# Attention and MLP in one kernel: the last chunk of w_out requested behind batch 1's normalise, batch 1's v ahead of it, and its products behind the kv products

## The chip, the cores and the metric

One core of a Trainium2 chip. The time is the device time of one execution in microseconds; below are medians of a few executions, and ratios are from runs of both kernels in the same rounds, so not quite the ratio of the medians that I quote. "First tile" is tokens 0 to 511, "tile 1" the next 512. Times inside a trace count from the start of its span. In the traces PE is TensorE, DVE VectorE, ACT ScalarE, POOL GpSimd and SP SyncE; "the clock" is the share of its full clock that TensorE was granted.

## The reference

Linear attention for 8 batches (8 heads, 576 positions, head dimension 64), then an MLP with a "snake" activation on the 4608 tokens:

```python
q_s = softmax(q, axis=-1);  k_s = softmax(k, axis=2)          # plain exp and sum in the kernel
kv  = einsum('bhsd,bhse->bhde', k_s, v)
x   = einsum('bhsd,bhde->bhse', q_s, kv)                      # -> (4608, 512)
h = x @ w_in                                                  # (4608, 2048)
g = h + sin(alpha * h)**2 / (alpha + 1e-9)
out = g @ w_out                                               # (4608, 512)
```

## The kernel before

Every tile of 512 tokens takes 64 products for `h`, an activation in between, and 64 products for `out`. In between stand the small attention products of the next batch. TensorE runs in program order; `take(os, n)` puts the next n of the first tile's 64 `out` products at that place in the order. w_out comes in four chunks of four blocks each; chunk c feeds products 16c+1 to 16c+16. It is cast from float32 to bfloat16 on its way and requested from GpSimd's queue; q, k and v come through Sync's.

```python
def load_wout(c):
    nc.gpsimd.dma_start(out=wout[:, 4*c:4*c+4, :], in_=wout_v[:, 4*c:4*c+4, :])
...
    GP_CP(win[:, :, 0:256], wf)              # first 256 columns of w_in, cast on GpSimd
...
late = {6: lambda: load("q", q, 1, halves=True, gate=DVE_CP), 8: lambda: load_wout(2),
        10: lambda: load_wout(3), 13: lambda: load("k", k, 1, halves=True, gate=DVE_CP)}
...                                          # 16 slots of the first tile; late[n] behind slot n
take(os, 10)
xp = ps_e.tile([128, 4, P], F32, name="xp", tag="a")
for c in range(4):
    attn_chunk(0, c, 8, 9, xp[:, c])
ACT_CP(xT[:, :, 8 * P:9 * P], xp)
take(os, 36)
exp_q(1)
load("v", v, 1, halves=True)
load_batch(2)                                # q, k, v of batch 2, Sync's queue
norm_q(1, [GP, V])                           # half on GpSimd, half on DVE
exp_k(1)
for ii in range(2):
    q_transpose(1, ii, ps_e, DVE_CP)         # TensorE, copies on DVE
cast_v(1, [ACT_CP, DVE_CP])
...
take(os, 8)
kv_mm(1, 0, ps_e, split=True)
kv_norm(1, 0, 1)
take(os, 2)
kv_mm(1, 1, ps_e, split=True)
kv_norm(1, 1, 2)
take(os, 1)
...                                          # two xp pairs with take(os, 2) behind each; the rest; tile 1
```

The softmax here doesn't subtract the row's maximum and nothing guards it: scores larger than these inputs give would overflow.

## Time and profile before

| | before |
|---|---|
| time, median (range) | 289.55 us (289.01 to 289.61) |
| span of the profiled run | 287.6 us |
| TensorE busy, mean granted clock | 95%, 0.997 |
| first tile's first w_in product / first w_out product | 16.23 / 30.05 us |
| last w_out chunk requested / landed | 28.40 / 38.76 us |
| batch 1's v landed (two halves) | 41.33, 42.71 us |
| tile 1's first w_in product | 47.76 us |

A busy TensorE is not a streaming one (each matmul's 379 ns overlap the next; the pitch of a 512-column product is 0.216 us), so gaps are read from start to start. Most of the lines are in the prediction; this is the one of tile 1:

```profile
47.76 3.62 PE L234 MATMUL hp<-xT,win 128*128 128x512 bf16 x16
```

### The profile page before, as it was taken

What the parts mean: (1) busy time and instruction counts of PE and PEld (TensorE: products, weight loads), DVE (VectorE), ACT (ScalarE), POOL (GpSimd) and SP (SyncE); (2) the same over time, 40 slices, a digit from 0 to 9 for tenths busy, and PEclk for the clock granted to TensorE, in tenths of its full rate; (3) what the DMA queues carried; (4) which work ended last, traced back from release to release, by engine and by line L of the source; (5) the groups of instructions that cost most, each with busy time, mean ns of one, the idle gap of its engine ahead of it and who ended that gap; (6) DMA issues with size and microseconds to landing.
All of it is one profiled execution on the core that took longest, in us unless ns stands there. A gap on an engine that the chain in (4) does not pass through costs nothing.

```text
span 287.6 us, 4234 instructions
## 1 busy us (share of the span) xinstructions
PE 273.7 (95%) x1542; PEld 130.8 (45%) x1570; DVE 188.6 (66%) x280; ACT 227.2 (79%) x321; POOL 79.8 (28%) x73
## 2 busy tenths in 40 slices
PE   2889999999999999999999999999999999999994
PEld 1434454445454445444544454445444444444443
DVE  3867595889958667856776677757674555555412
ACT  5799775999479999899889988998877777777500
POOL 0679420675775571005300440032000000000000
PEclk9999999999999999999999999999999999999998
DMA  7999999935899957129910990116011111111142
GB/s 257 341 205 245 267 401 407 309 150 161 196 153 404 392 187 128 38 43 368 275 32 22 331 333 8 38 39 136 19 39 36 36 36 39 36 38 36 46 103 73
DMA packets 37893, 46.03 MB, mean 160 GB/s; under 512 B 15968, under 2 KB 21360, under 8 KB 37872
## 3 DMA queue, kind: packets, MB, share of 16 engines
q1 hardware_dynamic: 33392, 41.69, 47.5%
q0 software_dynamic: 4288, 3.93, 8.4%
q8 instruction: 12, 0.20, 0.3%
q10 hardware_dynamic: 192, 0.14, 0.2%
q14 instruction: 9, 0.07, 0.1%
HBM read 36.71 MB, written 9.44 MB: 160 GB/s over the span
## 4 chain that ended last, share of the span: by engine, by line
PE 83%; DMA 5%; POOL 4%; DVE 3%; issue 2%; SPq 1%; ACT 1%; POOLq 0%
PE hp L234 36%; PE op L254 34%; PE hp L254 4%; DMA st_w<-in_moe_w_in_dram 3%; POOL s L244 3%; PE kvp L157 2%; PE xp L206 2%; PE hh L234 1%; DMA qT<-qn 1%; PE op L538 1%; PE op L234 1%; ACT s L240 1%; DVE g L250 1%; DVE qs L144 1%; SPq L94 1%
## 5 line engine op out<-in xcount | busy, mean ns | idle before, releaser
L250 DVE SCALAR_TENSOR_TENSOR g<-s,inva_sb,hp 128x512 bf16<-128x512 f32 x130 | 96.2, 746 | 64.2 <-ACT s L242 54.2
L234 PE MATMUL hp<-xT,win 128*128 128x512 bf16 x512 | 129.2, 379 | 1.2 <-POOL win L320 0.6
L254 PE MATMUL op<-wout,g 128*128 128x512 bf16 x479 | 121.9, 379 | 1.1 <-issue 0.5
L240 ACT ACTIVATE s<-hp,alpha_sb 128x512 f32<-128x512 f32 x130 | 87.7, 682 | 25.8 <-PE hp L234 25.0
L234 PEld LDWEIGHTS <-win 128*128 128x128 bf16 x576 | 56.1, 98 | 68.3 <-POOL win L320 1.1
L254 PEld LDWEIGHTS <-g 128*128 128x128 bf16 x560 | 54.1, 98 | 61.7 <-issue 0.8
L242 ACT ACTIVATE s<-s 128x512 f32<-128x512 f32 x112 | 70.5, 630 | 3.5
L146 POOL TENSOR_TENSOR qn<-qe,qs 128x1152 bf16<-128x1152 bf16 x12 | 25.3, 2126 | 74.3 <-DVE qs L140 63.1
L244 POOL TENSOR_TENSOR s<-s 128x512 f32<-128x512 f32 x29 | 30.5, 1062 | 22.2 <-ACT s L240 21.6
L260 DVE COPY o<-op 128x512 f32<-128x512 f32 (+2 forms) x33 | 22.1, 670 | 9.7 <-PE op L254 5.8
L117 ACT ACTIVATE ke<-st_k 128x1152 bf16<-128x1152 f32 x16 | 17.9, 1151 | 3.0 <-DMA st_k<-in_k_dram 3.0
L117 ACT ACTIVATE qe<-st_q 128x1152 bf16<-128x1152 f32 x16 | 17.8, 1155 | 2.4 <-DMA st_q<-in_q_dram 2.3
L139 DVE TENSOR_REDUCE qs<-qe 128x36 f32<-128x2304 bf16 x5 | 12.8, 2553 | 8.7 <-ACT qe L117 8.6
L131 POOL CAST vb<-st_v 128x1152 bf16<-128x1152 f32 x12 | 13.6, 1162 | 10.1 <-DMA st_v<-in_v_dram 10.1
L254 PE MATMUL hp<-wout,g 128*128 128x512 bf16 x62 | 14.8, 379 | 0.2 <-issue 0.2
L209 DVE CAST xT<-xp 128x512 bf16<-128x512 f32 (+1 forms) x18 | 13.4, 743 | 0.0
L144 DVE TENSOR_REDUCE qs<-qe 128x18 f32<-128x1152 bf16 x6 | 8.0, 1330 | 4.6 <-ACT qe L117 4.6
L157 PE MATMUL kvp<-vb,ke 64*128 64x130 bf16 x288 | 9.9, 217 | 0.3 <-ACT vb L310 0.3
L117 ACT ACT_TABLE_LOAD x7 | 9.0, 1283 | 1.3 <-PEq L552 1.2
L157 PEld LDWEIGHTS <-ke 64*128 64x128 bf16 x288 | 8.2, 93 | 3.9 <-ACT s L242 1.3
L234 PE MATMUL hh<-xT,win 128*128 128x512 bf16 x39 | 9.4, 379 | 0.1
L206 PE MATMUL xp<-qT,kbd 128*128 128x256 bf16 (+1 forms) x40 | 8.2, 286 | 0.4 <-DVE xT L209 0.3
(68 smaller groups left out, 117.3 us busy)
## 6 DMA issues: line engine op xcount, KB each, us to landing
out_dram<-o SPq DMA_DIRECT2D x70, 128.0 KB, 2.4
st_q<-in_q_dram SPq DMA_DIRECT2D x6, 1152.0 KB, 6.6
st_k<-in_k_dram SPq DMA_DIRECT2D x6, 1152.0 KB, 8.5
st_v<-in_v_dram SPq DMA_DIRECT2D x6, 1152.0 KB, 10.3
st_q<-in_q_dram SPq DMA_DIRECT2D x4, 576.0 KB, 5.1
st_k<-in_k_dram SPq DMA_DIRECT2D x4, 576.0 KB, 7.1
wout<-in_moe_w_out_dram POOLq DMA_DIRECT2D x4, 512.0 KB, 9.6
st_v<-in_v_dram SPq DMA_DIRECT2D x3, 576.0 KB, 9.2
```

The source lines that it names most:

```text
L117: nc.scalar.activation(dst[:, :, ii * 128:(ii + 1) * 128].rearrange("p j (x d) -> p x j d", x=2), src[:, ii::2], AX.Exp)
L131: engs[ii](vv[:, 2 * ii:2 * ii + 2, :, 0:D], staged["v", b][:, ii::2])
L146: engs[ii % len(engs)].tensor_tensor(qn[:, ii].rearrange("p j (x d) -> p j x d", x=2), qe[:, ii], part.unsqueeze(3).to_broadcast([128, J, ...
L157: nc.tensor.matmul(kvp[:, e, ii * 130:(ii + 1) * 130], ke[r, j, ii * 128:(ii + 1) * 128], vt[r, j, ii * 130:(ii + 1) * 130], start=(j == 0 ...
L206: nc.tensor.matmul(xp[:, e, 0:n], kt[:, e, ii], qT[:, ii, j0:j1, e * 64:(e + 1) * 64], start=True, stop=True)
L234: nc.tensor.matmul(hp, win[:, ki, ni * 128:(ni + 1) * 128], xT[:, ki, t * MF:(t + 1) * MF], start=(ki == 0), stop=(ki == 3))
L240: nc.scalar.activation(s, hp, AX.Sin, scale=alpha_sb[:, ni:ni + 1])
L242: nc.scalar.activation(s, s, AX.Square)
L244: nc.gpsimd.tensor_tensor(s, s, s, op=ALU.mult)
L250: nc.vector.scalar_tensor_tensor(G[t][:, ni], in0=s, scalar=inva_sb[:, ni:ni + 1], in1=hp, op0=ALU.mult, op1=ALU.add)
L254: nc.tensor.matmul(acc, G[t][:, ni, j * 128:(j + 1) * 128], wout[:, ni, :], start=(ni == 0), stop=(ni == nN - 1))
L260: eng(o[:, cols], acc)
```

## The change

Its author wanted batch 1's v, which the kv products need, ahead of the last w_out chunk in the memory traffic. The chunk's request therefore moves from slot 10 to behind the normalise on GpSimd, and its products move behind the kv products, to give it time. With it come three smaller parts: the w_in cast in two halves, 20 products in place of 10 ahead of the small `xp` group (whose copy goes to DVE), and v's cast ahead of the copies of qT on DVE.

```diff
-    GP_CP(win[:, :, 0:256], wf)
+    for n in range(2):
+        GP_CP(win[:, :, n * 128:n * 128 + 128], wf[:, :, n * 128:n * 128 + 128])
@@
-                10: lambda: load_wout(3), 13: lambda: load("k", k, 1, halves=True, gate=DVE_CP)}
+                13: lambda: load("k", k, 1, halves=True, gate=DVE_CP)}
@@
-        take(os, 10)
+        take(os, 20)
...
-        ACT_CP(xT[:, :, 8 * P:9 * P], xp)
-        take(os, 36)
+        DVE_CP(xT[:, :, 8 * P:9 * P], xp)
+        take(os, 26)
...
         norm_q(1, [GP, V])
+        load_wout(3)
         exp_k(1)
+        cast_v(1, [ACT_CP, DVE_CP])
         for ii in range(2):
             q_transpose(1, ii, ps_e, DVE_CP)
-        cast_v(1, [ACT_CP, DVE_CP])
...
-        take(os, 8)
-        kv_mm(1, 0, ps_e, split=True)
-        kv_norm(1, 0, 1)
         take(os, 2)
-        kv_mm(1, 1, ps_e, split=True)
-        kv_norm(1, 1, 2)
-        take(os, 1)
+        for ii in range(2):
+            kv_mm(1, ii, ps_e, split=True)
+            kv_norm(1, ii, ii + 1)
```

## The prediction

> **What bounds the kernel now.** I read the page first: share of each engine, then the chain that ended last.
>
> ```profile
> PE 273.7 (95%) x1542; PEld 130.8 (45%) x1570; DVE 188.6 (66%) x280; ACT 227.2 (79%) x321; POOL 79.8 (28%) x73
> ...
> PE 83%; DMA 5%; POOL 4%; DVE 3%; issue 2%; SPq 1%; ACT 1%; POOLq 0%
> ```
>
> TensorE carries the end. Busy is not peak, so I checked the pitch in the timeline: 512-column products start 0.216 us apart. From the first product of w_in (16.23) to the end, gaps over that pitch are few (those of exactly one pitch are lost records): 0.44 us before the `xp` products at 32.74, about 0.3 to 0.5 us each near 74 and 94 us. Nothing else is to be had after 16.2 us. So any new wait of TensorE adds in full, and the most that the change can win is what it takes out between 15 and 48 us. That stretch, in the timeline (start, length, instruction, idle before it and its releaser):
>
> ```profile
> 28.40 0.80 POOL L110 DMA_DIRECT2D wout<-in_moe_w_out_dram  x1
> ...
> 30.05 2.41 PE L254 MATMUL hp<-wout,g 128*128 128x512 bf16 x10
> ...
> 32.74 0.28 PE L214 MATMUL xp<-qT,kbd 128*128 128x64 bf16 x4 [0.28 <-DVE g L250]
> ...
> 32.86 7.93 PE L254 MATMUL hp<-wout,g 128*128 128x512 bf16 x35
> ...
> 35.94 1.35 DVE L144 TENSOR_REDUCE qs<-qe 128x18 f32<-128x1152 bf16 x1 [2.59 <-ACT qe L117]
> ...
> 37.76 2.13 POOL L146 TENSOR_TENSOR qn<-qe,qs 128x1152 bf16<-128x1152 bf16 x1 [5.33 <-DVE qs L145]
> ...
> 41.35 1.17 ACT L131 CAST vb<-st_v 128x1152 bf16<-128x1152 f32 x1 [0.20 <-DMA st_v<-in_v_dram]
> ...
> 43.49 0.69 PE L157 MATMUL kvp<-vb,ke 64*128 64x130 bf16 x18
> ...
> 46.68 1.24 PE L254 MATMUL hp<-wout,g 128*128 128x512 bf16 x5
> ```
>
> The reader is to see that the last chunk of w_out is requested at 28.40, and that the products of it (49 to 64 of the first tile) start about 42.1, well after it landed at 38.76. Tile 1's first w_in product is at 47.76. The DMA engines meanwhile are full (window sums; last columns clock, DMA share, GB/s):
>
> ```profile
> 33.00:35.00 2.00, 2.00 (x11) 0.87 (x9) 0.35 (x1) 1.91 (x3) 0.00 (x0) 1.00 1.23 219
> 38.00:40.00 2.00, 1.95 (x10) 0.90 (x10) 1.93 (x3) 1.18 (x2) 1.89 (x1) 1.00 1.05 411
> 42.00:44.00 2.00, 2.00 (x26) 1.00 (x23) 2.00 (x4) 1.97 (x3) 0.00 (x0) 1.00 1.04 412
> ```
>
> 219 GB/s is a stretch in which w_out (counted as written, in bf16) has the engines; 411 is q, k and v. They stay full until batch 2's v lands at 51.50. And what a w_out request takes from issue to landing:
>
> ```profile
> L110 POOL DMA_DIRECT2D wout<-in_moe_w_out_dram x4: 774/786/801, 17.3 to 28.4; - x4
> ...
> DMA to landing us min/median/max: 8.6/9.6/10.5
> ```
>
> **What the Trainium skill says.** "DMA: Bandwidth & Descriptors", Queues, rings and completion order: each DMA engine goes round-robin between queues, a packet at a time. The packet records agree once both queues are under way: from about 29.8 and again 34.9 us, packets of GpSimd's queue and of Sync's alternate one by one on an engine, a pair in 0.186 us. The same page (Latency and other measured facts) gives about 1 us to the first byte on GpSimd's path; here the first packet came 4.0 us after the issue began at 8.75, and about 4.1 us after the issue at 25.60, behind a full Sync queue both times, so I use 4.1. "TensorE: Matmul & The Clock Gate", Part 1: after an idle window of about 3.4 us TensorE falls to half clock and needs about 3.4 us of work to come back. The trace agrees: after the last product (283.9) the granted clock is 1.00 to 286 and 0.59 on average in 286 to 287 (half from 286.2), and the first warm-up matmuls (5.74 us on) have a pitch of 0.427 us, and 0.216 only from 9.7, 4.0 us later.
>
> **The change part by part.**
>
> (1) *w_in copy in two halves.* The 1024-element copy takes 1.04 us (15.13 to 16.17) and the 1152-element casts on GpSimd 1.16, so a half is about 0.55. The first product can start near 15.75, but the second (next in order) reads the second half and waits to about 16.3, against 16.46 now. Gain about 0.2 us.
>
> (2) *20 products ahead of `xp` in place of 10.* `xp` now waits for a buffer that the last combines free, 0.44 us. Ten more products are 2.16 us, past that wait. Together with 0.1 us of wait before product 10 (GpSimd no longer spends 0.80 us on the request at 28.40 ahead of its squares): gain about 0.5 us. The `xT` copy goes from ACT to DVE, so ACT's table load and batch 1's exps start some 2.2 us earlier; DVE's reduce waits behind the copy, whose input is ready at 29.87 + 20 x 0.216 + 0.1 + 0.2, about 34.5. Copy to 34.9, reduce and reciprocal to 36.5, GpSimd's normalise 36.7 to 38.8: 1.1 us earlier than now.
>
> (3) *Batch 1's k and v ahead of w_out.* Without the chunk's 32 packets per engine (32 x 0.0785 = 2.5 us) in front of them they land 1.5 to 3 us earlier. Worth nothing by itself: the cast of v waits 0.20 us today, and TensorE has products to fill with.
>
> (4) *The request of the last chunk, now at 38.8.* First packet 38.8 + 4.1 = 42.9. Sync's queue then still holds part of batch 2's k and all of its v, over 32 packets per engine, so they alternate: 32 x 0.186 = 6.0 us, 48.9; the three or four late engines and the completion add 0.4 to 0.9. Landing about 49.6. (At the queue's very end it would be about 51.3.)
>
> (5) *When its products are due.* TensorE: 29.87 + 46 x 0.216 + 0.1 = 39.9 (46 products), transposes 1.0, two products 0.4: 41.4. The kv products wait for v's second cast and both copies of qT on DVE, done near 42.5 to 43; kv, its normalise and the first `xp` pair end near 43.6 to 44.6. Then comes product 49, and everything in TensorE's order stands behind it. It waits until about 49.7, some 5.5 us.
>
> (6) *What is left then.* 16 products (3.45) and the second `xp` pair (0.38): tile 1 starts at 49.7 + 3.8 = 53.5 or a little over, in place of 47.76: +5.8 us. The gains of (1) and (2) are inside this, since the landing sets it, not TensorE.
>
> (7) *The clock.* An idle stretch of 5.5 us is over twice the 2.3 us after which the clock fell at the kernel's end. Coming back takes 4 us, as at the start, in which half the work gets done: +2.0 us, between 1 and 2.8 by the phase of the window. Behind that the kernel is TensorE-bound with the same program, so nothing comes back.
>
> Sum: 289.55 + 5.8 + 2.0 = 297.3; I take 297.0 for the few tenths that later waits may absorb.
>
> **The rivals.**
>
> *The wait never comes* (the change works as its author means it): then (1) and (2) give 289.55 - 0.7 = 288.9. It needs a landing by 44 us, 5.2 us after the request; the fastest w_out request took 8.6, and the DMA engines are no emptier then. Against it.
>
> *Landing sooner, by GpSimd's packets being served first:* 42.9 + 2.5 + 0.4 = 45.8, tile 1 at 49.7, +2.0 us, and perhaps no clock loss: 291.5 to 293. For it: between 31 and 34.5 us GpSimd's packets had the engines nearly alone. But Sync's request of that time was only just issued (31.17), and the alternation before and after speaks against it.
>
> *First come, first served:* all of batch 2 first, landing 51.3, +7.5 us and the clock: 299. For it: every request of the kernel before that was issued earlier also landed earlier, nearly so.
>
> *v becomes the bound:* the kv products now wait for DVE's cast and copies in series. At most 1 to 2 us of TensorE, and hidden by the wait for w_out.
>
> **Range and chances.** The order is certain from the program; the landing is the uncertain term (45.8 to 51.3), the clock the second. 10% for the first two rivals together, the rest between 294 and 299.5. 2% slower is 295.34, or +5.8, which the wait alone just reaches and wait plus clock exceed. Range 293.5 to 299.3; faster 0.02, same 0.20, slower 0.78.
>
> **What would show it.** In the profile after: the w_out request near 38.8 with its landing near 49 to 51; an idle stretch of TensorE of 4 to 7 us from about 44, ended by DMA of w_out; clock under 1.00 and a pitch of 0.427 for some 4 us after it; tile 1's first w_in product near 53.5 to 54; no wait before `xp`; k and v of batch 1 landed by 37 and 40 to 41. It is wrong if the chunk lands before 45 us, or if the clock stays at 1.00 through the wait: then about 295 or less.

## The result, and the profile after

The changed kernel took 298.36 us (298.07 to 298.68) against 289.31 of the kernel before in the same rounds: ratio 1.0313, 95% interval 1.0295 to 1.0331, slower. Its profiled span is 296.3 us, 8.7 more than before. On the page, the shares and the chain that ended last:

```profile
PE 277.6 (94%) x1570; PEld 131.6 (44%) x1570; DVE 189.0 (64%) x281; ACT 226.8 (77%) x320; POOL 79.8 (27%) x74
...
PE 81%; DMA 9%; DVE 3%; POOL 2%; issue 2%; SPq 1%; ACT 1%; POOLq 0%
```

DMA's share of the chain went from 5 to 9%. Where it entered, the chain in order of time between 36 and 58 us says (start, length, what):

```profile
37.26 2.07 POOL qn L146
39.33 11.31 DMA wout<-in_moe_w_out_dram
50.64 0.04 issue
50.69 1.01 PE hp L254 x2
51.70 0.75 PE xp L214 x2
52.44 4.17 PE hp L254 x14
56.61 1.51 PE hp L234 x7
```

GpSimd's normalise releases the request at 39.33, the chunk takes 11.31 us, and TensorE goes on with the two products behind it. The timeline of the same stretch shows the wait and what follows it:

```profile
34.79 0.28 PE L214 MATMUL xp<-qT,kbd 128*128 128x64 bf16 x4
...
39.10 1.17 ACT L131 CAST vb<-st_v 128x1152 bf16<-128x1152 f32 x1 [0.21 <-DMA st_v<-in_v_dram]
...
42.16 1.26 PE L157 MATMUL kvp<-vb,ke 64*128 64x130 bf16 x36
...
50.69 1.01 PE L254 MATMUL hp<-wout,g 128*128 128x512 bf16 x2 [6.38 <-DMA wout<-in_moe_w_out_dram]
...
52.24 4.37 PE L254 MATMUL hp<-wout,g 128*128 128x512 bf16 x14
...
56.45 3.62 PE L234 MATMUL hp<-xT,win 128*128 128x512 bf16 x16
```

The reader is to see four things. The `xp` group at 34.79 no longer waits. v's first half landed at 39.08 in place of 41.33, and the kv products start at 42.16 in place of 43.49: that part works as its author meant it. Then TensorE stands for 6.38 us. And the 14 products from 52.24 take 4.37 us where 14 at full pitch take some 3.2, though nothing holds them up. The window sums tell why (the third figure from the right is the granted clock):

```profile
44.00:46.00 2.00, 0.30 (x2) 0.05 (x1) 0.52 (x2) 0.91 (x1) 0.00 (x0) 1.00 1.13 287
46.00:48.00 2.00, 0.00 (x0) 0.00 (x0) 0.00 (x0) 0.00 (x0) 0.00 (x0) 0.95 1.10 284
48.00:50.00 2.00, 0.00 (x0) 0.00 (x0) 0.00 (x0) 0.00 (x0) 0.00 (x0) 0.50 1.09 336
50.00:52.00 2.00, 1.31 (x4) 0.53 (x4) 0.00 (x0) 0.00 (x0) 0.00 (x0) 0.50 0.48 186
52.00:54.00 2.00, 2.00 (x7) 0.66 (x6) 1.52 (x2) 0.00 (x0) 0.00 (x0) 0.50 0.00 0
54.00:56.00 2.00, 2.00 (x9) 0.83 (x8) 0.38 (x2) 0.58 (x1) 0.00 (x0) 0.84 0.28 63
```

The clock is at half from 47.81 to 54.64 us by its records. From 50.69 to 54.64 TensorE works at half speed: 3.95 us, in which it does 1.98 us of work. Engine columns of zero from 46 to 50 show that no engine of the core computes: all wait for this one transfer. The accounting of tile 1's start closes: 56.45 is the landing (50.64) plus 3.83 us of work behind it at full pitch plus 1.98; and 56.45 - 47.76 = 8.69 is the whole difference of the spans.

### The profile page after: what moved, and what is told of

Its sections match the earlier page's. It is cut to its first block, busy times and chain, and to the rows that moved or that the text cites. A ratio compares the mean times of both kernels' runs of the same rounds, so it can differ in the third digit from the quotient of the medians.

```text
span 296.3 us, 4263 instructions
## 1 busy us (share of the span) xinstructions
PE 277.6 (94%) x1570; PEld 131.6 (44%) x1570; DVE 189.0 (64%) x281; ACT 226.8 (77%) x320; POOL 79.8 (27%) x74
## 4 chain that ended last, share of the span: by engine, by line
PE 81%; DMA 9%; DVE 3%; POOL 2%; issue 2%; SPq 1%; ACT 1%; POOLq 0%
PE hp L234 36%; PE op L254 32%; DMA wout<-in_moe_w_out_dram 4%; DMA st_w<-in_moe_w_in_dram 3%; PE hp L254 3%; PE hh L234 3%; PE kvp L157 2%; PE xp L206 2%; DMA qT<-qn 1%; DVE qs L144 1%; PE op L537 1%; PE op L234 1%; POOL s L244 1%; ACT s L240 1%; POOL qn L146 1%
## 5 line engine op out<-in xcount | busy, mean ns | idle before, releaser
L254 PE MATMUL op<-wout,g 128*128 128x512 bf16 x496 | 124.2, 379 | 0.0
L254 PE MATMUL hp<-wout,g 128*128 128x512 bf16 x64 | 16.2, 408 | 6.4 <-DMA wout<-in_moe_w_out_dram 6.4
L260 ACT COPY o<-hp 128x512 f32<-128x512 f32 x2 | 1.2, 585 | 10.8 <-PE hp L254 10.8
```

The costliest lines, as they stand in the source:

```text
L254: nc.tensor.matmul(acc, G[t][:, ni, j * 128:(j + 1) * 128], wout[:, ni, :], start=(ni == 0), stop=(ni == nN - 1))
L260: eng(o[:, cols], acc)
```

## The experiments

Theory: the request comes so late, and meets so much other traffic, that its products stop TensorE, whose clock then falls. Rivals: the other parts of the change cost the time (v's cast ahead of the copies, the moved products and copies); or the wait alone does, and the clock is a bystander; or the chunk takes its 11 us whatever else is under way. Ten kernels ran, all with correct results.

**e1, the request back in slot 10, all else of the change kept.**

```diff
-                13: lambda: load("k", k, 1, halves=True, gate=DVE_CP)}
+                10: lambda: load_wout(3), 13: lambda: load("k", k, 1, halves=True, gate=DVE_CP)}
...
         norm_q(1, [GP, V])
-        load_wout(3)
```

> The changed kernel with the request of the last w_out chunk put back behind slot 10 of the first tile, everything else of the change kept. If the late request makes the loss: no wait for w_out, clock at 1.00 from 9.7 us to the end, and most of the 9.05 us gone. Not all of it: batch 1's v lands near 41.3 and 42.7 us again, as in the kernel before, while the new order casts it before the copies of qT, so the kv products wait about 2 us for that; 290 to 291.5 us. If the loss came from the other parts (v's cast before the copies, 20 products ahead, copies moved to DVE), the time stays above 295.

Measured: 293.63 us, ratio 1.0135 (1.0115 to 1.0155). The wait for w_out is gone, and so is about half of the loss; what remains is larger than I expected. v landed at 42.01 and 43.44, and TensorE waits 3.85 us instead of about 2:

```profile
43.47 0.76 DVE L131 CAST vb<-st_v 128x1152 bf16<-128x1152 f32 x1 [3.78 <-DMA st_v<-in_v_dram]
...
44.14 1.42 DVE L181 COPY qT<-tp 128x1152 bf16<-128x1152 bf16 x2
...
45.04 2.13 PE L157 MATMUL kvp<-vb,ke 64*128 64x130 bf16 x36 [3.85 <-DVE qT L181]
```

The cast that waits for v stands ahead of the copies that free the PSUM buffers of the kv products. That idle stretch also cost the clock (half from 44.05 to 50.88), and the 36 small products show it: 2.13 us, 1.26 in the changed kernel. (The profiled run is the slowest of the four; its mean clock was 0.988, that of the others 0.993 or 0.994.) The kernel of e8 below differs from this one only in the order of casts, copies and products, and took 289.52. So the new order is only good with an early v: a rival that is right for e1, and hidden in the changed kernel, where v is early.

**e2, the kernel before with the request alone moved.**

```diff
-                10: lambda: load_wout(3), 13: lambda: load("k", k, 1, halves=True, gate=DVE_CP)}
+                13: lambda: load("k", k, 1, halves=True, gate=DVE_CP)}
...
         norm_q(1, [GP, V])
+        load_wout(3)
```

> The kernel before with the request alone moved behind batch 1's normalise (its products stay where they were, ahead of the kv products). If the late request makes the loss: request near 39.9, landing near 51, TensorE idle from about 42.1 to 51 (9 us), behind it 16 products, both kv groups and both xp pairs (5.4 us) plus 2 us of half clock: tile 1 near 58.5, so about 300 us, slower than the whole change. If the order of the kv products and v's cast make the loss: within 2 us of the kernel before.

Measured: 299.03 us, ratio 1.0325 (1.0304 to 1.0346). One moved line of the program is enough for all of the loss. The chunk landed at 49.40, 10.4 us behind its request at 38.97; TensorE was idle for 8.03 us, and tile 1 started at 57.11:

```profile
49.44 2.72 PE L254 MATMUL hp<-wout,g 128*128 128x512 bf16 x6 [8.03 <-DMA wout<-in_moe_w_out_dram]
```

All other parts of the change together, the moving of the products behind the kv products among them, took back less than 1 us of it (299.03 to 298.36).

**e3, TensorE kept busy while it waits** (26 products that nothing reads).

```diff
             (ACT_CP, DVE_CP)[ii](xT[:, 2 * ii:2 * ii + 2, c0:c0 + 7 * P], xp)
+            if ii == 0:
+                keep = ps_e.tile([128, 2, 512], F32, name="keep", tag="a")
+                for _ in range(26):
+                    nc.tensor.matmul(keep[:, 0], identb, A["qe", 1][:, 0:4, 0:128], start=True, stop=True)
```

> The changed kernel with 26 dummy products (5.6 us at full clock) into a free PSUM tile while TensorE waits for w_out. If the half clock is a loss of its own: clock stays 1.00, the landing stays near 50.6, the products behind it at a pitch of 0.216, and the time falls by 2.0 us, to 296.4. If the wait alone makes the 9 us: no change, 298.4; if dummies delay it, more.

Measured: 296.0 us, ratio 1.0219 (1.02 to 1.0238): 2.4 us less than the changed kernel by the medians (1.9 between the two profiled spans), with added work. The landing did not move (50.51):

```profile
44.38 5.79 PE L423 MATMUL keep<-qe,identb 128*128 128x512 bf16 x26 [0.29 <-DVE kbd L170]
...
50.55 0.59 PE L254 MATMUL hp<-wout,g 128*128 128x512 bf16 x2 [0.39 <-DMA wout<-in_moe_w_out_dram]
...
51.36 3.19 PE L254 MATMUL hp<-wout,g 128*128 128x512 bf16 x14
```

The 14 products take 3.19 us, and the clock stays at 1.00. The half clock is a loss of its own, on top of the wait.

**e4, no other traffic beside the late chunk.**

```diff
         load("v", v, 1, halves=True)
-        load_batch(2)
...
         take(os)
+        load_batch(2)
         load("q", q, 3)
```

> The changed kernel with batch 2's q, k and v requested only behind the first tile's stores, so that no other packets share the DMA engines with the late w_out chunk. If a fixed time of about 4.1 us to the first packet and then one-by-one sharing make the 11.3 us: first packet still 4.1 us after the request (43.4), 32 packets per engine alone 2.5 us, landing near 46.4, wait about 2.3 us, time 291.5 to 294 by what the clock does. If the chunk stands in line behind the packets that are there (a depth of some 27 packets): landing near 44.2, next to no wait, 289 us. If the sharing doesn't matter: landing stays near 50.6 and the time at 298.4.

Measured: 291.21 us, ratio 1.0074 (1.0039 to 1.0109). The chunk landed at 44.53, 5.6 us behind its request in place of 11.3. Of the two accounts that I gave, the second holds for the landing (44.2 expected), though not for the time (289). By the packet records the first packet came 1.51 us after the request (38.95, 40.46) with the engines nearly empty, and 4.06 us after it (39.33, 43.39) in the changed kernel. So the 4.1 us are no fixed time: 2.55 us of them go when Sync's packets do, and I read them as a wait behind the packets already in line. At the rate of packets in the stretch ahead (184 per us, so one per engine in 0.087 us) that is some 29 packets per engine. Behind them, in the changed kernel, the chunk's 32 packets per engine alternate with as many of Sync's.

Other runs repeat both times: 4.07 us in e2 and 4.00 in e3, with the long queue; 1.50 in e9, without it. In e10 it was 1.59, though the engines moved 412 and 394 GB/s in the two us from 38 to 40: there Sync's queue was just running out (46 of its packets began in the 2 us behind that first packet, 174 in the changed kernel). So the long time goes with a long line, not with busy engines as such.

In e4 TensorE waited 0.58 us, and tile 1 started at 48.40. (Three of the four runs took 291.0 to 291.3; one took 293.2 at a mean clock of 0.991, and lifts the ratio.) The rest of the loss is new: TensorE stood 1.26 us at the second tile for transposes by DMA, against 0.17 before. The first of them took 5.6 us in place of 4.5, probably because batch 3's loads, pushed back by batch 2's, were longer on the engines:

```profile
76.32 0.32 PE L214 MATMUL hp<-qT,kbd 128*128 128x384 bf16 x1 [1.26 <-DMA qT<-qn]
```

**e5, the request ahead of the normalise** (behind the first tile's squares, 32.76).

```diff
         flush(lag, 0)
+        load_wout(3)
...
         norm_q(1, [GP, V])
-        load_wout(3)
```

> The changed kernel with the last w_out chunk requested right behind the first tile's squares (near 33 us), ahead of batch 1's normalise. If being late by some 6 us is all that is wrong: it lands near 43 to 44.5, about when its products are due, and no wait for w_out is left. But its 32 packets per engine then alternate with batch 1's k and v, so v lands near 42.5 in place of 40.6, and the kv products, whose copies stand behind v's cast, wait some 2 us: 291 to 293 us. If v's landing doesn't matter for the end: 288.7.

Measured: 294.13 us, ratio 1.0159 (1.0127 to 1.0191), a miss of 1 us on my upper figure. The chunk landed at 44.34, in time; but v, whose packets it now shared the engines with, landed at 42.07 and 44.14, 3.0 and 3.6 us later than in the changed kernel, and the kv products waited 3.65 us, behind which the clock was at half for 3.41 us. I had thought of a wait of 2. v does matter for the end, and the traffic is a sum: earlier for one is later for the other.

**e6, e7, e8, the parts that cost nothing, by themselves.** e6 is the kernel before with the cast in two halves; e7 the kernel before with 20 products and the copy on DVE; e8 both. (Diffs: the first and the third group of the change above.)

> The kernel before with the w_in copy in two halves and nothing else. If it works as predicted: about 0.1 to 0.2 us faster, so a ratio of 0.9995, hardly to be told from none. If two copies cost more than one: slower by up to 0.5 us.

> The kernel before with 20 products ahead of the single-column xp group (26 behind it) and its copy on DVE, nothing else. Prediction: the 0.44 us wait ahead of xp goes: 0.4 to 0.5 us faster, ratio 0.9985. If another wait takes its place (normalise behind the copy, transposes): no gain or a loss.

> The kernel before with the halves and the 20 products, the w_out request and the kv order left as before: the parts of the change that cost nothing. Prediction: 0.5 to 0.7 us faster than before, 288.8, ratio 0.998; it beats both kernels. If the parts of the change interact badly even without the late request: 289.4 or more.

Measured: 289.80 us, 289.17 and 289.52; ratios 1.0018 (0.9992 to 1.0045), 1.0000 (0.9974 to 1.0027) and 1.0006 (0.9976 to 1.0036). No gain is seen in any. The intervals are as wide as what was predicted (e8's reaches down to a gain of 0.7 us), so a small gain is not excluded; it is the traces that show why little is to be had. That of e7:

```profile
42.56 1.17 ACT L131 CAST vb<-st_v 128x1152 bf16<-128x1152 f32 x1 [0.62 <-DMA st_v<-in_v_dram]
...
43.77 0.69 PE L157 MATMUL kvp<-vb,ke 64*128 64x130 bf16 x18 [0.82 <-ACT vb L131]
```

The wait ahead of `xp` is gone, TensorE is at the kv products sooner, and waits there for v's cast, which waits for v. With the request in slot 10, v's first half landed between 41.28 (e8) and 42.62 (e6) from run to run: it is a second bound, as late as TensorE itself. In e8 the first kv product no longer waits, but the cast of v's second half (landed at 42.72) is in DVE's way: from the first kv product to tile 1 it takes 4.65 us, in e6 and e7 4.63, and 4.27 in the kernel before and in e10.

**e9, the change with batch 2 behind the late chunk.**

```diff
-        load_batch(2)
...
         for ii in range(2):
             q_transpose(1, ii, ps_e, DVE_CP)
+        load("q", q, 2, gate=DVE_CP)
+        load("k", k, 2)
+        load("v", v, 2)
```

> The changed kernel with batch 2's loads gated by DVE behind the copies of qT (near 42 us), so that they stand behind the late w_out chunk and are not as late as in e4. If the packets of batch 2 in line ahead of it and beside it were what made the chunk late: landing near 44.5 as in e4 (request 39, first packet 1.5 us later), wait about 0.7 us, and without e4's later loss of 1.1 us at the second tile: 290.0 us. If e4's time of 291.2 had another cause than late loads: 291 or more. If the gate does not hold them back: 298.

Measured: 290.32 us, ratio 1.0023 (1.0005 to 1.0042). Request 38.20, landing 43.96; no wait for w_out is left at product 49 (at 44.00), and tile 1 starts at 47.86. One gated load takes back 8 of the 9 us: v stays early (39.00 and 40.42), and the chunk has no line ahead of it. What is left is a wait for v's cast and the copies behind it:

```profile
42.02 1.26 PE L157 MATMUL kvp<-vb,ke 64*128 64x130 bf16 x36 [1.03 <-DVE qT L181]
```

**e10, e8 with the chunk in two halves.** Blocks 12 and 13 stay in slot 10; 14 and 15 go behind the normalise; batch 2 stands behind them as in e9.

```diff
+    def load_wout_half(h):
+        b = 12 + 2 * h
+        nc.gpsimd.dma_start(out=wout[:, b:b + 2, :], in_=wout_v[:, b:b + 2, :])
-                  [(n, m) for m in R for n in R]]
+                  [(n, m) for n in (0, 1) for m in R] + [(n, m) for m in R for n in (2, 3)]]
-                10: lambda: load_wout(3), 13: ...
+                10: lambda: load_wout_half(0), 13: ...
         norm_q(1, [GP, V])
+        load_wout_half(1)
```

> e8 with the last w_out chunk in two halves: blocks 12 and 13 requested in slot 10 as before, 14 and 15 behind the normalise, batch 2's loads gated behind them, and the chunk's products in that order. If v's landing, set by the sum of packets ahead of it, is what takes back the gain of the 20 products: v lands 1.2 us earlier (near 41.5), the kv products wait no longer, and it is 0.5 to 0.8 us faster than the kernel before (288.7, ratio 0.998). If the second half comes late (after 45 us) or the fuller queue order costs elsewhere: 289.5 or more.

Measured: 288.65 us (287.87 to 289.04) against 289.59, ratio 0.9970 (0.9951 to 0.9990): the one version that beats both kernels, by 0.3%. v landed at 40.30 and 41.77, the second half chunk at 42.99, ahead of its products. From the first tile's first w_out product to tile 1's first w_in product it takes 17.22 us, 17.71 in the kernel before: about what the 20 products were to gain, so it fits that this gain shows once v is early. It is not shown: two things were changed at once here (the halves, with the order of their products, and batch 2's place), and I did not part them.

## Why the prediction was right

It was right: 297.0 predicted, 298.36 measured, inside 293.5 to 299.3, and "slower" had 0.78. By its own steps:

- *(4), the landing.* Predicted request 38.8, first packet 42.9, landing 49.6; measured 39.33, 43.39 and 50.64. The request came 0.5 us later, most of it because that run's start did: w_in's first columns landed at 15.51 in place of 15.00, TensorE's first w_out product came at 30.48 in place of 30.05, and the copy, reduce and normalise behind it were late by as much. From request to landing it was 11.3 in place of 10.8: behind the 32 pairs (6.0 us, to 49.4) the last packets and the completion took 1.3 us in place of 0.4 to 0.9. The time to the first packet was right in size (4.06 for 4.1), and that was luck: I took it as a time of GpSimd's path, against the about 1 us to the first byte that the Trainium skill gives ("DMA: Bandwidth & Descriptors", Latency and other measured facts), and e4 shows 1.51 us without a queue and 2.55 that come with one. With another backlog, my 4.1 would have misled, as it would have in e4, e9 and e10.
- *(5), when the products are due:* 43.6 to 44.6 predicted; they began to wait at 44.3, for 6.38 us (5.5 predicted).
- *(6) and (7).* 5.8 us to tile 1's start and 2.0 for the clock were 6.7 and 2.0 in the trace (8.69 in all). e3 takes the clock's part away by itself and finds 2.4 by the medians, 1.9 by the spans. The 0.3 us that I took off for later waits was not there: from tile 1 to the end it is 239.8 us, 239.9 before.
- *(1), (2) and (3): this is the part that failed.* I wrote that k and v landing earlier is "worth nothing by itself" because the cast of v waits only 0.20 us, and gave (1) and (2) 0.7 us. e6 to e8 find none of it within their noise. v's landing caps it: once TensorE comes sooner, it waits for v (0.82 us in e7). The 0.20 us was also one profile's: with w_out's and v's requests as they were, v's first half landed up to 1.3 us later in other runs (42.62 in e6). A short wait of the cast meant that v was a bound just about to bite, not that it was slack; in the changed kernel v is early, and the landing of the late chunk sets the end, so none of this touched the total.
- *The rivals.* First come, first served fell: in the changed kernel, batch 2's v landed at 52.17, behind the chunk, though requested first (35.29). "GpSimd's packets first" fell with the one-by-one alternation. "v becomes the bound" was too small at 1 to 2 us: with v as late as in e1 and e5, the kv products waited 3.85 and 3.65 us. It was hidden, as I had said, because v was early.

Not settled: what a line of about 30 packets is, whether a depth per queue or something else; the size comes from one pair of runs, and the two requests of the kernel before that the prediction reads (4.0 and 4.1 us behind a full Sync queue) agree. And in e10, how much comes from the half chunk and how much from batch 2's place.

## What to carry to other kernels

A transfer moved "behind" something in a program is not just later by that much: it meets all the traffic that was requested meanwhile, so look at what is in line when it is issued, and move or gate the loads that nobody needs yet before you move one that is needed. Price a wait of TensorE by its length and, if it is long, by the half clock behind it: here every wait of 3.65 us or more between two stretches of work was followed by one, and none of 1.26 us or less was. And a wait of 0.2 us on a transfer is not slack: check where that transfer stands once the thing that hides it is gone.

## What the Trainium skill lacked or had wrong

- "DMA: Bandwidth & Descriptors", Queues, rings and completion order: round-robin a packet at a time between queues holds once a request is served (a pair in 0.186 us), but the page lacks that a new request can first stand behind packets of another queue: 1.51 us to the first packet with nearly empty engines, 4.06 with a full Sync queue. The about 1 us that the page gives to the first byte on GpSimd's path (Latency and other measured facts) was not reached in either.
- The same page's fit of 2.0 us plus bytes over 436 GB/s (Anatomy of one DMA) gives an estimate of 3.2 us for the 524288 bytes that a chunk writes, or of 4.4 us for the 1048576 bytes of float32 that it reads. The chunk took 5.6 us on nearly empty engines (e4). While such chunks ran, the engines wrote some 204 to 210 GB/s, against 410 with q, k and v; counted as read, in float32, that is about the same rate. The page gives no rate for transfers that cast, and doesn't say which side to count.
- "TensorE: Matmul & The Clock Gate", Part 1: its window of about 3.4 us fits (the half-clock stretches were 3.41, 6.83 and 10.24 us long, in e5, the changed kernel and e2, one to three windows), but its rule that the clock falls after at least one idle window is too mild: less than a whole idle window was enough. The clock fell 2.3 us after the last product at the end of the kernel before and 2.1 us into the wait of e2, and in e5 at 46.48, when TensorE had been at work again since 45.74.
